# Second-layer weight preparation during the first MLP: later and spread slots, loads ahead of decoding, out weights decoded in place

## The chip, the cores and the metric

One core of a Trainium2 chip runs the whole program. The metric is the device time of one execution in microseconds; lower is better.

## What is computed

A linear attention with a normalised output, and behind it two MLPs on the same 2304 tokens:

```python
def _attn_ref(q, k, v, g_norm):            # q, k, v: (4, 8, 576, 64)
    kv = np.einsum('bhsd,bhse->bhde', k, v)
    out = np.einsum('bhsd,bhde->bhse', q, kv)
    rms = np.sqrt(np.mean(out * out, axis=-1, keepdims=True) + 1e-06)
    return (out / rms * g_norm).astype(np.float32)

def _moe_ref(x, w_in, w_out):              # x: (2304, 512), w_in: (512, 2048)
    h = x @ w_in
    sp = np.where(h > 20.0, h, np.log1p(np.exp(np.minimum(h, 20.0))))
    return ((h * np.tanh(sp)) @ w_out).astype(np.float32)

def _moe2_ref(x, w_in, w_out, alpha):      # the second MLP
    h = x @ w_in
    g = np.maximum(h, 0.0) + alpha * np.minimum(h, 0.0)
    return (g @ w_out).astype(np.float32)
```

The weights arrive as 64-bit floating-point numbers. q, k, v and the output are float32.

## The kernel before

Every product is made of three fp32r matmuls (`three`, L125): high part by high part, high by low, low by high. So each operand is needed as a high part (a cast on ACT) and a low part (a subtraction on DVE).

**Slots.** The first MLP runs over five blocks of tokens (`BLOCKS`, 512, 256, 512, 512, 512) and 16 tiles j of the inner dimension, in NS = 80 slots; slot s is block s // 16, tile s % 16. In a slot PE makes the first product of s (`mm1`, 12 matmuls, tile h), ACT the Mish of s - 1 (`mish`, L502), ACT and DVE the two parts of its result (`g_split`, L495 and L496, tiles gh and gl) for s - 2, and PE the second product of s - 4 (`mm2`, 12 matmuls, tile acc). The attention of block i + 1 is strewn between these on half slots (`WHEN`, the dictionary `hook`): k by v, q by kv, mean squares, the rsqrt chain (`rsqrt_ev`, L319 to L330, 12 operations on DVE and one cast on ACT, tiles qT and yr), and `b_pe` (L336), which spreads yr over the partitions. PE's `b_pe` of blocks 2, 3 and 4 stands in slots 28, 44 and 60, and the chain starts two and a half to three slots before.

**The second MLP** runs in 96 quarters after slot 79 (slot NS + n is quarter n), three passes over 768 tokens of eight units each. A unit is two tiles j of the inner dimension, whose first product is computed with seven instead of eight block products, from sums and differences of the weights. Those, and all second-layer weights, are prepared while the first MLP runs:

- `load_w` loads a tile of 64-bit words into a stage buffer (512 KB). `w_scale` (L387, ACT) and `w_bits` (L393, L394 and L397, DVE) decode it to float32 in a buffer `wf` of which there are two.
- `prep_unit(i, step)`, in slots from `UNITS[i]` on: two decodes, four operations on 256 columns (L597 to L602), and five splits (`whole`, `high_low`, L572 and L573); the store of each result to a DRAM tile `wd` (`put`, L581) follows right behind it.
- `prep_out(j)`, in slot `OUTS[j]`: one decode, one split, one store.
- `fetch` (L624) brings the stored tiles back into the places of the first layer's weights when these have been used for the last time, `load_s` (L628) the sums and differences, unit by unit.

There are three stage buffers (tag `ws`, `stage`). They serve second-layer loads, the results of a unit (`wx`, two of them), the first MLP's results on their way to DRAM (`evac`, `xs`, two at each block's end) and the second MLP's inputs on their way back (`first_raw`, `xr`). `first_x` (L669 and on) splits these for the first pass, into tiles that `rooms1` takes from the two buffers of the tag `x`, which until then hold the blocks' inputs.

**What sets the order.** `add` puts a call into a dictionary under a slot, and `slot` runs `early`, `mm1`, `hook`, `after`, `late`, the rest of the slot's products, `mid`, `fin`, and at its end `last`. Up to slot 19 this order is the order of every queue. From slot 20 on only PE's order is written out; for ACT, DVE and SP, which issues every DMA, it is a priority, and a scheduler that runs when the program is built sets the order of each queue. Each queue then runs in that fixed order.

Of the kernel before, what the change touches and what calls it, by code (L numbers as in the profile page):

```python
# [25 lines left out]
P = 128  # L26
# [7 lines left out]
EARLY = 4  # L34
WHEN = {1: (8, 3, 1, 2, 3, 6), 2: (4, 4, 1, 2, 3, 6), 3: (0, 5, 1, 2, 4, 5), 4: (0, 5, 1, 2, 4, 5)}
MANUAL = 20
UNITS = (28, 31, 36, 39, 42, 45, 52, 55)
OUTS = (24, 25, 26, 27, 34, 48, 49, 50, 58, 59, 60, 61, 62, 63, 64, 65)
BY32 = 2
FIRST = "p0 c0 p1 c1 p2 p3 c2 c3 w4 u0 w5 u1".split()  # L40
START = """
# [8 lines left out]
def attn_moe_moe2(  # L50
# [89 lines left out]
    def room(nm, dt, cols):  # L140
        w, j = rooms.pop(0)
        return wp.tile([P, 2 * DM], dt, tag=f"w{w}{j}", name=nm)[:, :cols]
# [219 lines left out]
    def stage(nm, dt, cols):  # L362
        return st.tile([P, 2 * DM], dt, tag="ws", name=nm, bufs=3)[:, :cols]
# [3 lines left out]
    wst, wraw = {}, {}  # L367
    home = {}

    def load_w(L, which, j, early=False):  # L370


        s = room("ws", I32, 2 * DM) if early else stage("ws", I32, 2 * DM)
        if which == 2:
            nc.sync.dma_start(out=s, in_=wo[L][j * P : (j + 1) * P, :])
        elif which == 1:
            src = wi[L][:, 2 * j * P : 2 * (j + 1) * P].rearrange("(c p) f -> p c f", p=P)
            nc.sync.dma_start(out=s.rearrange("p (c f) -> p c f", c=NP), in_=src)
        else:
            nc.sync.dma_start(out=s, in_=wi[L][j * P : (j + 1) * P, : 2 * EARLY * P])  # L380
        wraw[L, which, j] = s
        words = s.rearrange("p (f w) -> p f w", w=2)
        wst[L, which, j] = words[:, :, 0], words[:, :, 1]
# [2 lines left out]
        high = f32(wst[L, which, j][1])  # L386
        nc.scalar.mul(high, high, 2.0**-112)  # L387

    def w_bits(L, which, j):
        low, high = wst[L, which, j]  # L390
        s = st.tile([P, DM], F32, tag="wf", name="wf")
        si = s.bitcast(I32)
        nc.vector.tensor_single_scalar(out=si, in_=low, scalar=29, op=ALU.logical_shift_right)  # L393
        nc.vector.scalar_tensor_tensor(  # L394
            out=si, in0=high, scalar=-0x80000000, in1=si, op0=ALU.bitwise_and, op1=ALU.bitwise_or
        )
        nc.vector.scalar_tensor_tensor(  # L397
            out=si, in0=high, scalar=3, in1=si, op0=ALU.logical_shift_left, op1=ALU.bitwise_or
        )
        wst[L, which, j] = s  # L400
# [178 lines left out]
    def put(nm, t):  # L579
        d = wd[nm] = dp.tile([P, t.shape[1]], F32, name="wd")  # L580
        nc.sync.dma_start(out=d, in_=f32(t))  # L581

    def prep_unit(i, step):

        j0, j1 = 2 * i, 2 * i + 1
        tt = nc.vector.tensor_tensor
        if step < 2:
            j = j0 + step
            w_scale(1, 1, j)
            w_bits(1, 1, j)  # L590
            return
        sa, sb = wst[1, 1, j0], wst[1, 1, j1]
        r0, r1 = wraw[1, 1, j0], wraw[1, 1, j1]
        s1, s3 = (f32(r1)[:, n * QW : (n + 1) * QW] for n in range(2))
        a11, a12, a21, a22 = sa[:, :QW], sa[:, QW:], sb[:, :QW], sb[:, QW:]
        if step == 2:
            tt(out=s1, in0=a21, in1=a22, op=ALU.add)  # L597
            tt(out=s3, in0=a11, in1=a21, op=ALU.subtract)
            tt(out=a21, in0=s1, in1=a11, op=ALU.subtract)
            whole(r0, sa)  # L600
            put((1, j0), r0)
            tt(out=a12, in0=a12, in1=a21, op=ALU.subtract)  # L602
            high_low(*halves(r1, 1), s1)
            put(("s", i, 1), r1[:, 2 * QW :])
        else:
            x = stage("wx", I32, 2 * DM)
            high_low(*halves(x, 0), s3)
            put(("s", i, 0), x[:, : 2 * QW])
            high_low(*halves(x, 1), a12)
            put(("s", i, 2), x[:, 2 * QW :])  # L610
            x = stage("wx", I32, 2 * DM)
            whole(x, sb)
            put((1, j1), x)

    def prep_out(j):
        w_scale(1, 2, j)
        w_bits(1, 2, j)
        r = wraw[1, 2, j]
        whole(r, wst[1, 2, j])
        put((2, j), r)  # L620

    def fetch(which, j):
        h, l = w_home(1, which, j)
# [185 lines left out]
    def add(d, s, f, *a):  # L809
        d.setdefault(s, []).append((f, a))  # L810
# [35 lines left out]
    for j in range(NJ):  # L846
        if j >= EARLY and (1, j) not in early_w:
            add(late, max(j - 3, EARLY), load_w, 0, 1, j)
            add(mid, j - 2, w_begin, 0, 1, j)
        if (2, j) not in early_w:  # L850
            add(early, max(j + 1, EARLY), load_w, 0, 2, j)
            add(last, j + 2, w_begin, 0, 2, j)
            add(mid, j + 3, w_end)
        add(early, NS - NJ + max(j, EARLY) + 1, fetch, 1, j)
        add(early, NS + 2 * j - 3, fetch, 2, j)
    for i, s in enumerate(UNITS):
        for step in range(4):
            add(fin, s + step - step // 2, prep_unit, i, step)
        for n in range(2):
            add(last, s - 1, load_w, 1, 1, 2 * i + n)  # L860
    for j, s in enumerate(OUTS):
        add(fin, s, prep_out, j)
        add(last, s - 1, load_w, 1, 2, j)
    add(early, NS - NJ + 4, rooms1)
    for n in range(2):
        add(early, NS - 6 + 3 * n, first_raw, n)
        add(fin, NS - 5 + 3 * n, first_x, n)
    add(early, NS, rooms2)
    for n in range(3):
        add(early, NS, load_s, 0, n)  # L870
# [158 lines left out]
```

## Time and profile before

| | |
|---|---|
| median of three runs | 905.21 us (898.15 to 906.84) |
| the profiled execution | 907.59 us, of which span 905.8 us |
| PE busy | 849.1 us, 94% |
| DVE busy | 551.7 us, 61% |
| ACT busy | 318.0 us, 35% |
| mean granted TensorE clock | 0.976 |

The span runs from the first to the last instruction of one profiled execution; the rest of its time lies around it. Busy shares are means over stages that differ much. A wait is put down to the instruction that ended it. `ws<-in_moe_w_in_dram` reads: tile ws is written from the weights in DRAM; SPq is the queue that issues DMAs. The granted clock is a share of 2.4 GHz; TensorE runs either at that or at 1.2 GHz.

### The profile page before, as it was taken

What the parts mean: (1) busy time and instruction counts of PE and PEld (TensorE: products, weight loads), DVE (VectorE), ACT (ScalarE), POOL (GpSimd) and SP (SyncE); (2) the same over time, 40 slices, a digit from 0 to 9 for tenths busy, and PEclk for the clock granted to TensorE, in tenths of its full rate; (3) what the DMA queues carried; (4) which work ended last, traced back from release to release, by engine and by line L of the source; (5) the groups of instructions that cost most, each with busy time, mean ns of one, the idle gap of its engine ahead of it and who ended that gap; (6) DMA issues with size and microseconds to landing.
All of it is one profiled execution on the core that took longest, in us unless ns stands there. A gap on an engine that the chain in (4) does not pass through costs nothing.

```text
span 905.8 us, 11722 instructions
## 1 busy us (share of the span) xinstructions
PE 849.1 (94%) x4408; PEld 721.4 (80%) x4408; DVE 551.7 (61%) x1062; ACT 318.0 (35%) x619; POOL 1.3 (0%) x7
## 2 busy tenths in 40 slices
PE   7999889868996999959999999999999999999997
PEld 5677678757875788748888888888889888898886
DVE  6988864685548826682251355557855559655554
ACT  4766444544454435442242211112311114211111
POOL 0000000000000000000000000000000000000000
PEclk9999999969999999979999999999999999999999
DMA  9676446946574615650485641232412132211211
GB/s 263 182 201 178 134 117 172 258 159 147 165 237 151 184 61 198 243 187 24 160 284 195 209 151 48 57 91 62 128 47 59 47 117 59 104 59 48 59 47 70
DMA packets 89352, 121.37 MB, mean 134 GB/s; under 512 B 35280, under 2 KB 59344, under 8 KB 89296
## 3 DMA queue, kind: packets, MB, share of 16 engines
q1 hardware_dynamic: 89296, 120.62, 43.3%
q8 instruction: 35, 0.57, 0.3%
q14 instruction: 21, 0.17, 0.1%
HBM read 88.09 MB, written 32.51 MB: 133 GB/s over the span
## 4 chain that ended last, share of the span: by engine, by line
PE 65%; DMA 16%; DVE 12%; ACT 3%; SPq 2%; issue 2%; DVEq 0%; ACTq 0%
PE acc L129 11%; PE acc L127 11%; PE acc L128 11%; PE pp L127 6%; PE pp L129 6%; PE pp L128 6%; PE h L127 4%; PE h L128 4%; PE h L129 4%; DMA ws<-in_moe_w_in_dram 3%; DMA ws<-in_moe_w_out_dram 3%; DMA wd<-wx 3%; DMA wd<-ws 2%; DMA xr<-x2d 2%; DMA q<-in_q_dram 2%
## 5 line engine op out<-in xcount | busy, mean ns | idle before, releaser
L127 PE MATMUL acc<-gh,w 128*128 128x512 f32 (+1 forms) x320 | 122.5, 383 | 0.9 <-ACT n L502 0.4
L128 PE MATMUL acc<-gl,w 128*128 128x512 f32 (+1 forms) x320 | 120.5, 376 | 0.0
L129 PE MATMUL acc<-gh,w 128*128 128x512 f32 (+1 forms) x320 | 120.4, 376 | 0.0
L127 PE MATMUL h<-x,w 128*128 128x512 f32 (+1 forms) x240 | 93.7, 391 | 12.0 <-ACT n L502 12.0
L496 DVE TENSOR_TENSOR gl<-n,gh 128x512 fp32r<-128x512 f32 (+1 forms) x80 | 50.7, 633 | 82.4 <-ACT gh L495 82.3
L129 PE MATMUL h<-x,w 128*128 128x512 f32 (+1 forms) x240 | 90.9, 379 | 0.4 <-DVE w L436 0.3
L128 PE MATMUL h<-x,w 128*128 128x512 f32 (+1 forms) x240 | 90.7, 378 | 0.0
L129 PE MATMUL acc<-w,g 128*128 128x512 f32 x216 | 85.6, 396 | 0.2
L734 ACT CAST g<-ty 128x384 fp32r<-128x384 f32 x48 | 24.7, 514 | 150.0 <-DVE ty L732 140.9
L127 PEld LDWEIGHTS acc<-gh,w 128*128 128x128 f32 x320 | 62.6, 196 | 12.3 <-ACT n L502 0.9
L495 ACT CAST gh<-n 128x512 fp32r<-128x512 f32 (+1 forms) x80 | 46.1, 576 | 72.6 <-PE acc L129 72.1
L129 PEld LDWEIGHTS acc<-gh,w 128*128 128x128 f32 x320 | 62.3, 195 | 10.9 <-DVE w L436 0.4
L128 PEld LDWEIGHTS acc<-gl,w 128*128 128x128 f32 x320 | 62.6, 196 | 10.1
L127 PEld LDWEIGHTS h<-x,w 128*128 128x128 f32 x240 | 47.1, 196 | 25.7 <-ACT n L502 15.5
L387 ACT ACTIVATE ws<-ws 128x512 f32<-128x512 f32 x64 | 43.6, 683 | 54.7 <-DMA ws<-in_moe_w_in_dram 28.1
L128 PE MATMUL acc<-w,xb 128*128 128x512 f32 x144 | 56.8, 395 | 0.0
L128 PE MATMUL acc<-w,g 128*128 128x512 f32 x144 | 56.8, 395 | 0.0
L393 DVE TENSOR_SCALAR wf<-ws 128x512 int32<-128x512 int32 x64 | 27.1, 424 | 48.3 <-DMA ws<-in_moe_w_in_dram 24.9
L502 ACT ACTIVATE n<-h 128x512 f32<-128x512 f32 (+1 forms) x80 | 44.4, 555 | 33.2 <-DVE gl L496 32.4
L127 PE MATMUL acc<-w,g 128*128 128x512 f32 x144 | 56.0, 389 | 0.0
L127 PE MATMUL acc<-w,xb 128*128 128x512 f32 x144 | 56.0, 389 | 0.0
L129 PEld LDWEIGHTS h<-x,w 128*128 128x128 f32 x240 | 47.1, 196 | 9.4 <-DVE w L436 1.6
(183 smaller groups left out, 1702.4 us busy)
## 6 DMA issues: line engine op xcount, KB each, us to landing
xb<-wd SPq DMA_DIRECT2D x72, 256.0 KB, 2.7
ws<-in_moe_w_in_dram SPq DMA_DIRECT2D x32, 512.0 KB, 4.3
ws<-in_moe_w_out_dram SPq DMA_DIRECT2D x32, 512.0 KB, 4.1
w<-wd SPq DMA_DIRECT2D x28, 512.0 KB, 3.6
wd<-ws SPq DMA_DIRECT2D x24, 512.0 KB, 2.7
k<-in_k_dram SPq DMA_DIRECT2D x16, 288.0 KB, 4.6
v<-in_v_dram SPq DMA_DIRECT2D x16, 288.0 KB, 4.9
out_dram<-osb SPq DMA_DIRECT2D x18, 256.0 KB, 2.2
```

The lines of the kernel that those rows point to most:

```text
L127: nc.tensor.matmul(ps, lh, rh, start=start, stop=False, **kw)
L128: nc.tensor.matmul(ps, lh, rl, start=False, stop=False, **kw)
L129: nc.tensor.matmul(ps, ll, rh, start=False, stop=stop, **kw)
L387: nc.scalar.mul(high, high, 2.0**-112)
L393: nc.vector.tensor_single_scalar(out=si, in_=low, scalar=29, op=ALU.logical_shift_right)
L495: nc.scalar.copy(out=gh, in_=g)
L496: nc.vector.tensor_tensor(out=gl, in0=g, in1=f32(gh), op=ALU.subtract)
L502: nc.scalar.activation(out=g, in_=hps.pop(kk)[:, :T], func=AF.Mish)
L734: nc.scalar.copy(out=h, in_=out)
```

## The change

It moves the preparation of the second layer's weights and takes one part of it out of DRAM.

- Units are spread: `UNITS` starts at slots 36, 41, 46, 52, 57, 62, 65 and 70 instead of 28 to 55. The loads of a unit's two tiles stand in slots s and s + 1 (`late`, in the middle of the slot), their decodes in s + 1 and s + 2, the rest in s + 2 to s + 4, each store one slot after what it stores. Before, both loads stood at the end of slot s - 1 and the work in s to s + 2.
- A unit uses three stage buffers instead of four uses of them: the split of its second tile goes where that of its first was (`place`). Units 6 and 7 use neither stage buffers nor `wf`, but one of the two buffers of tag `x` (`late_places`); `rooms1` moves from slot 68 to 75, the first pass's input loads from 74 and 77 to 75 and 77, its splits from 75 and 78 to 76 and 78.
- Out tiles are loaded into the place where the second MLP reads them, once the first layer's tile there has been used (`load_out`, from slot 70 on), and decoded there two slots later (`prep_w`). There is no store and no fetch for them, and eight of the sixteen come after slot 80. `OUTS` and `prep_out` go.

```diff
@@ -34,8 +34,8 @@
 EARLY = 4
 WHEN = {1: (8, 3, 1, 2, 3, 6), 2: (4, 4, 1, 2, 3, 6), 3: (0, 5, 1, 2, 4, 5), 4: (0, 5, 1, 2, 4, 5)}
 MANUAL = 20
-UNITS = (28, 31, 36, 39, 42, 45, 52, 55)
-OUTS = (24, 25, 26, 27, 34, 48, 49, 50, 58, 59, 60, 61, 62, 63, 64, 65)
+SOON = 6
+UNITS = (36, 41, 46, 52, 57, 62, 65, 70)
 BY32 = 2
 FIRST = "p0 c0 p1 c1 p2 p3 c2 c3 w4 u0 w5 u1".split()
 START = """
@@ -367,10 +367,10 @@
     wst, wraw = {}, {}
     home = {}
 
-    def load_w(L, which, j, early=False):
-
-
-        s = room("ws", I32, 2 * DM) if early else stage("ws", I32, 2 * DM)
+    def load_w(L, which, j, early=False, s=None):
+
+
+        s = s if s is not None else room("ws", I32, 2 * DM) if early else stage("ws", I32, 2 * DM)
         if which == 2:
             nc.sync.dma_start(out=s, in_=wo[L][j * P : (j + 1) * P, :])
         elif which == 1:
@@ -386,9 +386,9 @@
         high = f32(wst[L, which, j][1])
         nc.scalar.mul(high, high, 2.0**-112)
 
-    def w_bits(L, which, j):
+    def w_bits(L, which, j, s=None):
         low, high = wst[L, which, j]
-        s = st.tile([P, DM], F32, tag="wf", name="wf")
+        s = s if s is not None else st.tile([P, DM], F32, tag="wf", name="wf")
         si = s.bitcast(I32)
         nc.vector.tensor_single_scalar(out=si, in_=low, scalar=29, op=ALU.logical_shift_right)
         nc.vector.scalar_tensor_tensor(
@@ -580,17 +580,36 @@
         d = wd[nm] = dp.tile([P, t.shape[1]], F32, name="wd")
         nc.sync.dma_start(out=d, in_=f32(t))
 
+    places, late_places = {}, {}
+
+    def place(i, nm):
+
+        if (i, nm) not in places:
+            if i < SOON:
+                t = stage(nm, I32, 2 * DM) if nm in ("r0", "r1", "x") else st.tile([P, DM], F32, tag="wf", name="wf")
+            else:
+                if not late_places:
+                    t = xp.tile([P, 8 * TM], I32, tag="x", name="xw")
+                    for n, to in enumerate(("r0", "r1", "x")):
+                        late_places[to] = t[:, 2 * n * DM : 2 * (n + 1) * DM]
+                    for n, to in enumerate("ab"):
+                        late_places[to] = f32(t[:, (6 + n) * DM : (7 + n) * DM])
+                t = late_places[nm]
+            places[i, nm] = t
+        return places[i, nm]
+
+    def load_unit(i, n):
+        load_w(1, 1, 2 * i + n, s=place(i, f"r{n}"))
+
     def prep_unit(i, step):
 
-        j0, j1 = 2 * i, 2 * i + 1
+        if step < 2:
+            j = 2 * i + step
+            w_scale(1, 1, j)
+            w_bits(1, 1, j, place(i, "ab"[step]))
+            return
         tt = nc.vector.tensor_tensor
-        if step < 2:
-            j = j0 + step
-            w_scale(1, 1, j)
-            w_bits(1, 1, j)
-            return
-        sa, sb = wst[1, 1, j0], wst[1, 1, j1]
-        r0, r1 = wraw[1, 1, j0], wraw[1, 1, j1]
+        sa, sb, r0, r1 = (place(i, nm) for nm in ("a", "b", "r0", "r1"))
         s1, s3 = (f32(r1)[:, n * QW : (n + 1) * QW] for n in range(2))
         a11, a12, a21, a22 = sa[:, :QW], sa[:, QW:], sb[:, :QW], sb[:, QW:]
         if step == 2:
@@ -598,26 +617,28 @@
             tt(out=s3, in0=a11, in1=a21, op=ALU.subtract)
             tt(out=a21, in0=s1, in1=a11, op=ALU.subtract)
             whole(r0, sa)
-            put((1, j0), r0)
+        elif step == 3:
+            x = place(i, "x")
             tt(out=a12, in0=a12, in1=a21, op=ALU.subtract)
             high_low(*halves(r1, 1), s1)
+            high_low(*halves(x, 0), s3)
+            high_low(*halves(x, 1), a12)
+        else:
+            whole(r0, sb)
+
+    def put_unit(i, step):
+        r0, r1, x = (places.get((i, nm)) for nm in ("r0", "r1", "x"))
+        if step == 0:
+            put((1, 2 * i), r0)
+        elif step == 1:
             put(("s", i, 1), r1[:, 2 * QW :])
+            put(("s", i, 0), x[:, : 2 * QW])
+            put(("s", i, 2), x[:, 2 * QW :])
         else:
-            x = stage("wx", I32, 2 * DM)
-            high_low(*halves(x, 0), s3)
-            put(("s", i, 0), x[:, : 2 * QW])
-            high_low(*halves(x, 1), a12)
-            put(("s", i, 2), x[:, 2 * QW :])
-            x = stage("wx", I32, 2 * DM)
-            whole(x, sb)
-            put((1, j1), x)
-
-    def prep_out(j):
-        w_scale(1, 2, j)
-        w_bits(1, 2, j)
-        r = wraw[1, 2, j]
-        whole(r, wst[1, 2, j])
-        put((2, j), r)
+            put((1, 2 * i + 1), r0)
+
+    def load_out(j):
+        load_w(1, 2, j, s=wp.tile([P, 2 * DM], I32, tag=f"w2{j}", name="ws"))
 
     def fetch(which, j):
         h, l = w_home(1, which, j)
@@ -852,19 +873,20 @@
             add(last, j + 2, w_begin, 0, 2, j)
             add(mid, j + 3, w_end)
         add(early, NS - NJ + max(j, EARLY) + 1, fetch, 1, j)
-        add(early, NS + 2 * j - 3, fetch, 2, j)
+        t0 = NS - 10 + 3 * j // 2 if j < 8 else NS + 2 * (j - 7)
+        add(early, t0, load_out, j)
+        add(fin, t0 + 2, prep_w, 1, 2, j)
     for i, s in enumerate(UNITS):
-        for step in range(4):
-            add(fin, s + step - step // 2, prep_unit, i, step)
-        for n in range(2):
-            add(last, s - 1, load_w, 1, 1, 2 * i + n)
-    for j, s in enumerate(OUTS):
-        add(fin, s, prep_out, j)
-        add(last, s - 1, load_w, 1, 2, j)
-    add(early, NS - NJ + 4, rooms1)
+        add(late, s, load_unit, i, 0)
+        add(late, s + 1, load_unit, i, 1)
+        for step in range(5):
+            add(fin, s + (1, 2, 2, 3, 4)[step], prep_unit, i, step)
+        for step in range(3):
+            add(late, s + 3 + step, put_unit, i, step)
+    add(early, NS - 5, rooms1)
     for n in range(2):
-        add(early, NS - 6 + 3 * n, first_raw, n)
-        add(fin, NS - 5 + 3 * n, first_x, n)
+        add(early, NS - 5 + 2 * n, first_raw, n)
+        add(fin, NS - 4 + 2 * n, first_x, n)
     add(early, NS, rooms2)
     for n in range(3):
         add(early, NS, load_s, 0, n)
```

## Rows read from the trace of the kernel before

**Rows 1.** The page's first line.

```profile
span 905.8 us, 11722 instructions
```

**Rows 2.** Busy by stretch: us; PE, weights, DVE, ACT, POOL busy (x); clock; DMA share, GB/s.

```profile
124.74:156.75 32.01, 31.00 (x252) 27.12 (x250) 17.13 (x31) 15.65 (x36) 0.00 (x0) 1.00 0.49 119
156.75:233.51 76.76, 59.70 (x419) 53.49 (x417) 48.32 (x95) 34.81 (x79) 0.00 (x0) 0.87 0.66 186
233.51:316.94 83.43, 75.04 (x362) 59.35 (x361) 59.94 (x114) 40.06 (x79) 0.00 (x0) 0.96 0.60 190
316.94:422.04 105.10, 94.59 (x409) 76.50 (x408) 59.68 (x106) 46.19 (x83) 0.00 (x0) 0.95 0.44 154
422.04:509.28 87.24, 87.24 (x385) 71.99 (x384) 23.23 (x40) 27.23 (x48) 0.00 (x0) 1.00 0.57 192
509.28:590.00 80.72, 80.72 (x401) 72.43 (x400) 44.05 (x83) 15.09 (x29) 0.00 (x0) 1.00 0.33 102
620.00:660.00 40.00, 39.61 (x195) 34.97 (x194) 33.39 (x68) 15.67 (x31) 0.00 (x0) 1.00 0.29 92
```

**Rows 3.** PE's waits, 156.75 to 233.51: total us, times, longest.

```profile
PE bps L336 <- DVE yr L330: 7.8, 1, 7.8
PE h L127 <- ACT n L502: 6.1, 4, 2.4
```

**Rows 4.** The same, 233.51 to 316.94.

```profile
PE bps L336 <- DVE yr L330: 5.1, 1, 5.1
```

**Rows 5.** The same, 316.94 to 422.04.

```profile
PE bps L336 <- DVE yr L330: 9.3, 1, 9.3
```

**Rows 6.** DVE's busy time in the windows of two rsqrt chains.

```profile
276.00:294.00 18.00, 15.77 (x31) 0.94 0.52 179
...
379.50:400.00 20.50, 17.54 (x32) 0.86 0.62 218
```

**Rows 7.** The same for tile qT alone, the chain's operations.

```profile
276.00:294.00 18.00, 8.02 (x12) 0.94 0.52 179
...
379.50:400.00 20.50, 8.02 (x12) 0.86 0.62 218
```

**Rows 8.** Groups by line in these windows: xcount | busy, mean ns | idle before.

```profile
L393 DVE TENSOR_SCALAR wf<-ws 128x512 int32<-128x512 int32 x2 | 0.9, 428 | 2.1 <-DMA ws<-in_moe_w_in_dram 2.1
...
L393 DVE TENSOR_SCALAR wf<-ws 128x512 int32<-128x512 int32 x4 | 1.7, 426 | 3.0 <-DMA ws<-in_moe_w_out_dram 3.0
```

**Rows 9.** DVE's timeline: start, us, instruction, idle before it.

```profile
284.00 0.43 DVE L393 TENSOR_SCALAR wf<-ws 128x512 int32<-128x512 int32 x1 [1.09 <-DMA ws<-in_moe_w_in_dram]
284.35 0.68 DVE L325 SCALAR_TENSOR_TENSOR qT<-qT 128x512 f32<-128x512 f32 x1
```

**Rows 10.** Groups by line, whole run.

```profile
L394 DVE SCALAR_TENSOR_TENSOR wf<-ws,wf 128x512 int32<-128x512 int32 x64 | 44.2, 690 | 6.7 <-ACT ws L387 3.7
...
L393 DVE TENSOR_SCALAR wf<-ws 128x512 int32<-128x512 int32 x64 | 27.1, 424 | 48.3 <-DMA ws<-in_moe_w_in_dram 24.9 <-DMA ws<-in_moe_w_out_dram 23.3
...
L573 DVE TENSOR_TENSOR ws<-wf,ws 128x512 fp32r<-128x512 f32 x24 | 16.5, 688 | 3.2 <-ACT ws L572 3.0
...
L597 DVE TENSOR_TENSOR ws<-wf 128x256 f32<-128x256 f32 x8 | 3.4, 421 | 0.1
```

**Rows 11.** DMA issues of the page: count, KB each, median us to landing.

```profile
ws<-in_moe_w_in_dram SPq DMA_DIRECT2D x32, 512.0 KB, 4.3
ws<-in_moe_w_out_dram SPq DMA_DIRECT2D x32, 512.0 KB, 4.1
```

**Rows 12.** Waits of the whole run, DVE's decode for its loads.

```profile
DVE wf L393 <- DMA ws<-in_moe_w_in_dram: 24.9, 14, 4.9
...
DVE wf L393 <- DMA ws<-in_moe_w_out_dram: 23.3, 11, 7.4
```

**Rows 13.** SP's timeline: start, us, issues.

```profile
319.66 0.38 SPq L378 DMA_DIRECT2D ws<-in_moe_w_in_dram  x1
...
443.12 0.68 SPq L665 DMA_DIRECT2D xr<-x2d  x1
```

## The prediction

> **What bounds the kernel now.** I read the span first, and then a table of PE by stretches that I cut at the starts of slots, found in the timeline as the first product of a slot: 124.74 is slot 16, 156.75 slot 23, 233.51 slot 36, 316.94 slot 48, 422.04 slot 64, 509.28 the first product of the second MLP. I call the stretches A to F [rows 2]. The reader is to see three columns there: PE's busy time against the length, DVE's, and the granted clock.
>
> E is what an undisturbed stretch looks like: 16 slots in 87.24 us with PE busy for all of it and the clock at 1.00, so a slot of 512 tokens takes 5.45 us. A is nearly as clean, 1.0 us idle in 32.0. B, C and D are not. I count as lost there the idle time and the share of the stretch that the clock did not grant (a mean of 0.87 says that 13% of the cycles of the upper level, 2.4 GHz, were missing; the two overlap a little, so this is a slight overestimate). B: 76.76 - 59.70 = 17.1 idle and 0.13 x 76.76 = 10.0 of clock, 27 us. C: 8.4 and 3.3, 11.7 us. D: 10.5 and 5.3, 15.8 us. Together 54.5 of the 905.8 us span [rows 1]. The change can only work on these 54.5 us: it removes no work from PE.
>
> Next I asked who ended PE's waits. One wait of 7.8 us in B, one of 5.1 us in C and one of 9.3 us in D are the same place, b_pe (L336), waiting for yr (L330), the end of the rsqrt chain of blocks 2, 3 and 4 [rows 3 to 5]. In B another 6.1 us are the first layer's product waiting for Mish, the longest 2.4 us [rows 3]. So DVE and ACT are late, not PE, and the clock that B, C and D lose follows those idle stretches.
>
> Why is yr late? Between 276 and 294 us DVE spent 8.02 us on the 12 operations of the chain, but 15.77 us on everything; between 379.5 and 400 us 8.02 of 17.54 us [rows 6, 7]. The rest is almost all decoding of second-layer weights, placed between the chain's operations: L393 at 284.00, then L325 of the chain right behind it [rows 9]. And L393 stood in line for its load: 2.1 us in the first of these windows, 3.0 us in the second [rows 8]. DVE works in its order, so the chain waits as well. Over the whole run L393 waited 48.2 us in 25 waits for loads, 1.9 us each [rows 12].
>
> **What the change does, part by part.**
>
> *Work.* Nothing leaves DVE or ACT. A weight tile's decode stays L393, L394, L397 (the last is of the same kind and size as L394) and a split: 0.42 + 2 x 0.69 + 0.69 = 2.5 us of DVE for an out tile. A unit is two decodes (3.6 us), two splits at full width (1.4) and seven operations on 256 columns (7 x 0.42 = 2.9): 7.9 us of DVE [rows 10]. What goes away is DMA: 16 stores of decoded out tiles and their 16 fetches, with 16 uses of the three shared stage buffers. PE waits for none of these fetches where it waits long [rows 3 to 5], so their price on the path is zero; what they occupied is the buffers, SP's queue and bandwidth.
>
> *Where the work goes.* Units leave slots 28 to 57 for 36 to 74, outs leave 24 to 65 for 72 to 98. B (slots 23 to 35) held four outs, units 0 and 1 and a fifth out, and is left with at most the first load and decode of unit 0. So in B the chain stands alone. It needs 8 us, and the three slots of 256 tokens between its first operation and b_pe give about that (3 x 5.45 / 2 = 8.2); the 7.8 us wait falls away, and with it the 2.4 us wait for Mish and the clock lost after them. I keep A's idle rate (1.0 / 32.0 of 76.76 us, 2.4 us) and the other 3.7 us of waits for Mish, which stand around the loads of q and not only around the decodes. 27.1 - 6.1 = 21 us gained in B. Ends: 27 if those waits go too, 15 if the clock's share comes back only by half and 1 us of the chain's wait stays.
>
> *C and D.* Here I don't take the new slot numbers at their word. They order the work, but only PE's order is written out; on the other queues a step starts when its buffer is free. first_raw is listed for slot 74 and its first load issued at 443.12, in slot 67 (438.4 to 443.8 by 5.45 us a slot); a unit's load listed for slot 51 issued at 319.66, in slot 48 [rows 13]. So I expect units 0 to 2 to follow each other from slot 36 as fast as three buffers allow, and units 3 to 5 from slot 52, and both later chains (slots 41 to 44 and 57 to 60) to meet a unit again. What gets better: loads stand further ahead of decodes, so I take off L393's waits in those windows, 2.1 of the 5.1 us in C and 3.0 of the 9.3 us in D. In D a unit also replaces outs running back to back, and DVE's other work shrinks towards that of C: (17.54 - 8.02) - (15.77 - 8.02) = 1.8 us. With the clock in proportion to the idle time that makes 2.1 x (1 + 3.3 / 8.4) = 2.9 us in C and 4.8 x (1 + 5.3 / 10.5) = 7.2 us in D. Ends: nothing in either, and all but 1 us of each, 10.7 and 14.8.
>
> A load takes 4.3 and 4.1 us in the median to land [rows 11], within a slot of 5.45, but the waits [rows 8, 12] show that the issue came too late for that. The Trainium skill's page "DMA: Bandwidth & Descriptors", section "Anatomy of one DMA", gives 2.0 us and the bytes over 436 GB/s for another queue than SP's; an estimate by it is 3.2 us for 512 KB. By that rule half a slot of lead is enough, a longer one buys nothing, and the sum would lose the DMA part of C and D, 2.9 and 4.5 us, for a time near 885. The loads here are slower than the rule and the waits are there, so I go by the trace.
>
> *Puts and order on SP.* The puts come a slot after what they store. SP then waits less for DVE, and the loads behind a put issue sooner; this is in the 2.1 and 3.0 us above. A unit now uses three stage buffers and writes its last split over the first, so that split waits for a store to land, on DVE; nothing but the unit needs it, and its slot (s + 4) is two behind the store's work.
>
> *E and F pay.* Three units less what runs ahead, some eight outs and first_x come into E, where DVE is busy 23.23 of 87.24 us: 3 x 7.9 + 8 x 2.5 = 44 us more, 77%. E has no rsqrt chain. Units 6 and 7 hold an x buffer, so the split of the second MLP's inputs cannot run as early as it did; it must now fit between the last store of unit 7 and slot 80, and what is late next would be the second MLP's first products. The other eight outs, 20 us of DVE, come into the second MLP, which is busy 44.05 of 80.72 us there: 64 of 81, 79%. The nearest row is 620 to 660, DVE 33.39 of 40.00 us, PE idle 0.4 us in 40 [rows 2]. By that F loses 0.8 us. If the cover of E and F were gone, each of 22 loads would cost PE its 1.9 us, 42 us and more with the clock. I take 3 us, near the row: 1 in F, 2 for the transition.
>
> **Sum.** 21 + 2.9 + 7.2 - 3 = 28 us. The profiled execution took 907.59 us, 905.8 of span and 1.8 around it; the median of the runs is 2.4 us lower, 905.2. So 879.6 for an execution like the profiled one, and 877 on the median.
>
> **Rivals.**
>
> 1. *All comes back* (0.20). The units do spread as listed, a chain meets one decode at most, and the two and a half slots from its first operation to b_pe (13.6 us) are enough. B + C + D: 21 + 10.7 + 14.8 - 3 = 43 us, 862. For it: the chain alone needs 8 of these 13.6 us. Against it: issues that run ahead of their slots [rows 13].
> 2. *The later chains are as late as before* (0.14). Units from slots 36 and 52 crowd DVE as they did, loads are late again, and only B gains: 21 - 3 = 18, 887. For it: DVE in C, where only units ran and it was busy for 15.77 us of 18 [rows 6].
> 3. *The other side: E and F become what B was* (0.07). Decodes wait for their loads in front of operations that PE needs soon. One such wait costs 1.9 us and, with B's clock over idle time, 1.9 x (1 + 10.0 / 17.1) = 3.0 us. From ten of them on (31 us of gain over 3.0) the change is slower; 16, one for each out, give 905 - 31 + 48 = 922. Against it: E without idle time, and two slots of lead.
> 4. *It doesn't do what it says* (0.09). The scheduler puts each decode right behind its load again, B fills with work pulled forward (attention's loads, unit 0), and what is gained in one chain is lost at the transition: 905.
>
> **How the numbers follow.** The forecast has 0.50, with a range of its own from 868 to 886. Left out may be 0.2: I leave out most of 3 and 4 and the far end of 1, and get 856 to 896. This kernel's three runs reach from 898 to 907, so about 1% (9 us) is what can be told from no change. Faster by over 1% (below 896): forecast, 1 and 2, 0.84 less a little for their upper ends, 0.83. Within 1%: 4 and the mild end of 3, 0.10. Slower: 0.07.
>
> **What would show it.** Right, if PE's wait at L336 in slot 28 is under 1 us and the clock there stays near 1.00; if slots 23 to 35 take about 56 us instead of 76.76; if the waits at L336 in slots 44 and 60 are there but under 3 and 5 us; if L393's waits for loads fall well below 48 us; if there is no store or fetch of out tiles, and PE is idle less than 4 us more in slots 64 to 98. Wrong, if the waits in slots 44 and 60 are as long as before (rival 2) or gone (rival 1), or if PE waits in the first quarters of the second MLP for operations that stand behind a decode (rival 3).

## The result, and the profile after

The median falls from 904.33 us (898.15 to 906.84, four runs) to 870.04 us (869.05 to 872.79, four runs): a ratio of 0.964, 95% interval 0.961 to 0.968, 34.3 us less. The profiled execution took 872.79 us. The page's first line and its row of the granted clock:

```profile
span 870.8 us, 11649 instructions
...
PEclk9999899999999999999999999999999999999999
```

The same row of the kernel before:

```profile
PEclk9999999969999999979999999999999999999999
```

The span is 35.0 us shorter than in [rows 1], and the two slices in which the clock had been low, around 190 and 396 us, are full; the 8 that stands now belongs to 87 to 109 us, in the first block's slots, which the change doesn't touch. Busy time by stretch, cut at the same slots as [rows 2] (slots 16, 23, 36, 48, 64, the second MLP's first product): us; PE, weights, DVE, ACT, POOL busy (x); clock; DMA share, GB/s. The stretches are A, B, C, D, E, and the last is the second MLP's first 80.72 us:

```profile
126.73:160.38 33.65, 31.10 (x251) 27.12 (x249) 18.25 (x33) 16.04 (x37) 0.00 (x0) 1.00 0.53 116
160.38:214.63 54.25, 51.70 (x419) 47.22 (x417) 24.83 (x44) 21.69 (x54) 0.00 (x0) 1.00 0.29 63
214.63:293.11 78.48, 74.26 (x362) 58.83 (x360) 47.72 (x87) 32.90 (x66) 0.00 (x0) 0.98 0.45 143
293.11:387.02 93.91, 92.54 (x410) 75.04 (x409) 49.50 (x89) 39.91 (x74) 0.00 (x0) 1.00 0.30 101
387.02:474.68 87.66, 87.66 (x385) 71.85 (x384) 60.46 (x113) 45.50 (x83) 0.00 (x0) 1.00 0.72 254
474.68:555.40 80.72, 79.81 (x394) 71.11 (x393) 53.94 (x103) 21.47 (x40) 0.00 (x0) 1.00 0.31 102
```

B is 22.5 us shorter, C 5.0, D 11.2; E is as long as it was, with DVE busy for 60.46 us of it instead of 23.23; and the second MLP from its first product to the end took 396.2 us, before 396.5. Against that stand 2.0 us more up to slot 16 and 1.6 us more in A, where nothing was changed. 22.5 + 5.0 + 11.2 - 3.6 = 35.1, the span's difference but for rounding.

PE's waits of the whole run (total us, times, longest):

```profile
PE h L127 <- ACT n L502: 7.5, 8, 1.9
PE bps L336 <- DVE yr L330: 5.3, 3, 2.1
```

The three waits at b_pe were 7.8, 5.1 and 9.3 us [rows 3 to 5]; now they are 1.9 in slot 28, 2.1 in slot 44 and 1.3 in slot 60. The chains of blocks 3, 4 and 2, in this order, from their first operation to the end of yr, before and then after (columns as above; a chain is 12 operations of DVE):

```profile
276.48:293.30 16.82, 9.64 (x42) 7.30 (x40) 14.61 (x29) 6.41 (x13) 0.00 (x0) 0.95 0.53 180
379.68:399.80 20.12, 9.66 (x42) 7.34 (x40) 17.16 (x32) 7.96 (x14) 0.00 (x0) 0.86 0.62 218
175.66:194.30 18.64, 8.74 (x59) 8.33 (x57) 16.35 (x33) 7.33 (x16) 0.00 (x0) 0.77 0.53 167
```

```profile
259.77:271.30 11.53, 9.34 (x40) 7.07 (x39) 11.22 (x21) 4.52 (x10) 0.00 (x0) 1.00 0.33 126
355.66:366.85 11.19, 9.85 (x43) 7.50 (x41) 10.87 (x20) 4.23 (x8) 0.00 (x0) 1.00 0.32 119
172.88:183.40 10.52, 8.73 (x72) 8.53 (x72) 9.20 (x15) 3.10 (x8) 0.00 (x0) 1.00 0.01 2
```

The two later chains took 16.8 and 20.1 us with 15 and 18 foreign operations between their own, and now take 11.5 and 11.2 with 8 and 7 (the counts of these windows hold one or two more, at the edges). That of block 2 took 18.6 us and takes 10.5, with three operations of `g_split` left in it and no unit. DVE's timeline shows where the foreign operations stand in block 3's chain (start, us, instruction):

```profile
259.77 0.69 DVE L319 TENSOR_SCALAR qT<-msps 128x512 f32<-128x512 f32 x1
260.38 0.42 DVE L618 TENSOR_TENSOR wf<-r,wf 128x256 f32<-128x256 f32 x1
260.71 0.42 DVE L573 TENSOR_TENSOR r<-r 128x256 fp32r<-128x256 f32 x1
...
263.25 0.42 DVE L573 TENSOR_TENSOR x<-wf,x 128x256 fp32r<-128x256 f32 x1
263.59 0.69 DVE L325 SCALAR_TENSOR_TENSOR qT<-qT 128x512 f32<-128x512 f32 x1
...
270.52 0.75 DVE L330 SCALAR_TENSOR_TENSOR yr<-yr,neglo,qT 128x512 fp32r<-128x512 f32 x1
```

Up to 263.6 the end of unit 2 alternates with the chain as a unit did before; from there on the chain meets only two of `g_split`'s operations (L496). SP's timeline says why (start, us, issues):

```profile
248.12 1.83 SPq L378 DMA_DIRECT2D r<-in_moe_w_in_dram  x2
...
274.84 6.45 SPq L180 DMA_DIRECT2D q<-in_q_dram  x8
281.33 0.49 SPq L378 DMA_DIRECT2D r<-in_moe_w_in_dram  x1
...
317.97 0.37 SPq L378 DMA_DIRECT2D r<-in_moe_w_in_dram  x1
```

Unit 2's loads, listed for slots 46 and 47, issued in slot 41, so its decode fell on the chain. Unit 3's first load came only in slot 45, behind the chain. Unit 2's stores had all landed by 267.0 us, but in SP's queue eight loads of q stood in front of it, which had waited for DVE (L243). Nothing else was there to decode: the outs that once filled this room now issue from slot 69 on.

### The profile page after: what moved, and what is told of

Same layout as the page of the kernel before. It is cut to its first block, busy times and chain, and to the rows that moved or that the text cites. A ratio compares the mean times of both kernels' runs of the same rounds, so it can differ in the third digit from the quotient of the medians.

```text
span 870.8 us, 11649 instructions
## 1 busy us (share of the span) xinstructions
PE 840.4 (97%) x4408; PEld 714.1 (82%) x4408; DVE 554.5 (64%) x1062; ACT 316.3 (36%) x619; POOL 1.3 (0%) x7
## 4 chain that ended last, share of the span: by engine, by line
PE 70%; DVE 14%; DMA 9%; ACT 3%; issue 2%; SPq 1%; DVEq 0%; ACTq 0%
PE acc L128 11%; PE acc L127 11%; PE acc L129 11%; PE pp L127 6%; PE pp L129 6%; PE pp L128 6%; PE h L127 5%; PE h L128 5%; PE h L129 5%; DMA r<-in_moe_w_in_dram 3%; DMA v<-in_v_dram 2%; DVE wf L394 2%; DVE wf L397 2%; PE kvps L211 1%; DMA wd<-x 1%
## 5 line engine op out<-in xcount | busy, mean ns | idle before, releaser
L127 PE MATMUL acc<-gh,w 128*128 128x512 f32 (+1 forms) x320 | 120.8, 377 | 0.6 <-ACT n L502 0.4
L129 PE MATMUL acc<-gh,w 128*128 128x512 f32 (+1 forms) x320 | 118.8, 371 | 0.0
L127 PE MATMUL h<-x,w 128*128 128x512 f32 (+1 forms) x240 | 91.7, 382 | 5.8 <-ACT n L502 5.7
L129 PE MATMUL h<-x,w 128*128 128x512 f32 (+1 forms) x240 | 89.8, 374 | 0.7 <-DVE w L436 0.7
L128 PE MATMUL h<-x,w 128*128 128x512 f32 (+1 forms) x240 | 89.3, 372 | 0.0
L496 DVE TENSOR_TENSOR gl<-n,gh 128x512 fp32r<-128x512 f32 (+1 forms) x80 | 50.7, 634 | 44.4 <-ACT gh L495 44.0
L127 PEld LDWEIGHTS acc<-gh,w 128*128 128x128 f32 x320 | 61.0, 190 | 11.9 <-ACT n L502 0.9
L129 PEld LDWEIGHTS acc<-gh,w 128*128 128x128 f32 x320 | 60.9, 190 | 10.8 <-DVE w L436 0.4
L495 ACT CAST gh<-n 128x512 fp32r<-128x512 f32 (+1 forms) x80 | 46.1, 576 | 52.9 <-PE acc L129 52.3
L127 PEld LDWEIGHTS h<-x,w 128*128 128x128 f32 x240 | 45.6, 190 | 18.9 <-ACT n L502 8.7
L129 PEld LDWEIGHTS h<-x,w 128*128 128x128 f32 x240 | 45.7, 191 | 9.4 <-DVE w L436 1.6
L128 PEld LDWEIGHTS h<-x,w 128*128 128x128 f32 x240 | 45.7, 190 | 7.2
L129 PEld LDWEIGHTS acc<-w,g 128*128 128x128 f32 x216 | 40.5, 188 | 9.6 <-DVE g L756 1.1
```

The source lines that it names most:

```text
L127: nc.tensor.matmul(ps, lh, rh, start=start, stop=False, **kw)
L128: nc.tensor.matmul(ps, lh, rl, start=False, stop=False, **kw)
L129: nc.tensor.matmul(ps, ll, rh, start=False, stop=stop, **kw)
L495: nc.scalar.copy(out=gh, in_=g)
L496: nc.vector.tensor_tensor(out=gl, in0=g, in1=f32(gh), op=ALU.subtract)
```

## Experiments

Three theories stood. *The lead*: loads stand ahead of decodes, so DVE waits less in front of the chain. *The chains' company*: what counts is which foreign operations stand between a chain's operations, whoever put them there. *The amount*: slots 23 to 63 simply held too much preparation of all kinds, and any thinning helps. (What an expectation calls its theory and its rival, it says itself.) The lengths below are differences between the starts of first products in the profiled executions; the medians are of all runs, and before is taken anew beside each group (904.8, 903.7 and 902.9 us). A profiled execution can lie off its median: that of 5 is the slowest of six (894.6 us), those of 6 (863.1) and of the kernel after (872.8) the slowest of four. Where the intervals of two kernels overlap, the medians alone don't tell them apart.

| kernel | median us | ratio, 95% | B | C | D | E | F |
|---|---|---|---|---|---|---|---|
| before | 904.3 | | 76.8 | 83.4 | 105.1 | 87.2 | 396.5 |
| after | 870.0 | 0.961 to 0.968 | 54.3 | 78.5 | 93.9 | 87.7 | 396.2 |
| 1 outs at home, old units | 887.6 | 0.978 to 0.984 | 67.1 | 81.5 | 92.1 | 87.6 | 397.2 |
| 2 the same, new unit slots | 869.7 | 0.959 to 0.968 | 55.4 | 74.6 | 94.1 | 87.1 | 400.6 |
| 3 after, no lead | 867.9 | 0.956 to 0.962 | 54.3 | 74.9 | 94.1 | 88.1 | 398.2 |
| 4 after, units behind chains | 862.6 | 0.951 to 0.957 | 54.4 | 73.1 | 92.0 | 87.8 | 396.6 |
| 5 before, all behind chains | 887.6 | 0.978 to 0.984 | 64.1 | 84.2 | 99.2 | 92.2 | 394.9 |
| 6 as 4, b_pe of block 2 later | 860.1 | 0.950 to 0.955 | 51.7 | 72.2 | 92.0 | 88.1 | 397.2 |
| 7 after, 8 outs decoded twice | 873.4 | 0.964 to 0.969 | 55.8 | 77.4 | 94.3 | 88.0 | 401.3 |
| 8 after, two units decoded twice | 876.4 | 0.968 to 0.973 | 54.7 | 80.2 | 96.4 | 88.3 | 396.6 |
| 9 before, L387 on GpSimd | 904.3 | 1.000 to 1.004 | 73.5 | 85.3 | 105.2 | 87.0 | 395.3 |
| 10 as 5, L387 on GpSimd | 887.9 | 0.981 to 0.986 | 63.8 | 84.8 | 98.2 | 87.2 | 395.4 |
| 11 as 6, L387 on GpSimd | 867.7 | 0.958 to 0.963 | 51.7 | 74.5 | 92.0 | 89.9 | 400.8 |

**1. Only the outs.** The kernel before, with second-product weights loaded to their place and decoded there late; units as they were.

```diff
...
+    def load_out(j):
+        load_w(1, 2, j, s=wp.tile([P, 2 * DM], I32, tag=f"w2{j}", name="ws"))
...
-        add(early, NS + 2 * j - 3, fetch, 2, j)
+        t0 = NS - 10 + 3 * j // 2 if j < 8 else NS + 2 * (j - 7)
+        add(early, t0, load_out, j)
+        add(fin, t0 + 2, prep_w, 1, 2, j)
...
-    for j, s in enumerate(OUTS):
-        add(fin, s, prep_out, j)
-        add(last, s - 1, load_w, 1, 2, j)
```

> The kernel before with one part of the change: out tiles are loaded and decoded in place, late; units keep their old slots, loads and four stage uses. Theory (work in front of the rsqrt chains): the outs leave stretches B and D, units 0 and 1 stay in B. PE's wait at L336 in slot 60 goes (9.3 us before) with its clock, some 13 us; B gains some 5 us from the outs that stood before slot 28; the waits in slots 28 and 44 stay at 3 to 8 us. About 886 us (880 to 893). Rival (DMA traffic and stage buffers are what costs, and this part takes away all the traffic that the change takes away): as the whole change, 870 to 874. Rival (the lead of the loads): nothing of it is in this kernel, over 898.

PE's waits at b_pe, whole run:

```profile
PE bps L336 <- DVE yr L330: 11.7, 2, 6.6
```

6.6 us in slot 28, 5.1 in slot 44, none in slot 60. Half of the gain, 17 of 34 us, is the outs', 13 us of the profiled execution's in D, where outs had stood in the chain of block 4, and 10 in B. The rival, by which the traffic that is gone brings the whole gain, is refuted; but decodes, traffic and buffers of the outs go together here, and this run does not part them. C keeps its wait, as it should: units 2 to 5 still fill it.

**2. New unit slots besides.** One line more; a unit's loads, its four buffers and its steps as before.

```diff
-UNITS = (28, 31, 36, 39, 42, 45, 52, 55)
+UNITS = (36, 41, 46, 52, 57, 62, 68, 71)
```

> Outs in place as in the first run, and units in the new slots (36, 41, 46, 52, 57, 62, then 68 and 71), but with the old unit: both loads in the slot before the first decode, stores right behind the work, four uses of the three stage buffers. Theory (where the work stands is what counts): B is clear, 868 to 876, at most 5 us over the changed kernel since a unit with four buffer uses takes longer and meets the chain of slot 44 for longer. Rival (lead, stores a slot later and three buffers carry the gain of the later stretches): 880 to 888.

```profile
PE bps L336 <- DVE yr L330: 5.0, 3, 1.9
```

The other half: 869.7, B and C 12 and 7 us shorter than in experiment 1. This kernel has the old lead, one slot, and the old units, and is as fast as the change. Its second MLP took 400.6 us, some 4 us more than in the kernel after; that was not followed up.

**3. No lead.** The kernel after, with loads listed in the slot of their decode.

```diff
-        add(early, t0, load_out, j)
+        add(early, t0 + 2, load_out, j)
...
-        add(late, s, load_unit, i, 0)
-        add(late, s + 1, load_unit, i, 1)
+        add(late, s + 1, load_unit, i, 0)
+        add(late, s + 2, load_unit, i, 1)
```

> The changed kernel with every load of a unit and of an out tile listed in the slot of its own decode instead of one or two slots before. Theory (slots only order the work, a load issues when its buffer is free, so the listed lead hardly moves the issues): as the changed kernel, 868 to 873, decodes wait for loads as long as there. Rival (the lead is what keeps decodes from standing in front of the chains): L393's waits for loads go up by 1 to 2 us each and the time to 876 to 885.

SP's timeline, the loads of units 2 (both) and 3:

```profile
241.42 1.82 SPq L378 DMA_DIRECT2D r<-in_moe_w_in_dram  x2
...
273.07 0.49 SPq L378 DMA_DIRECT2D r<-in_moe_w_in_dram  x1
...
309.71 0.37 SPq L378 DMA_DIRECT2D r<-in_moe_w_in_dram  x1
```

Counted in slots that is 41, 45.9 and 52.3, the very places of the kernel after. Here the listed slot doesn't set the issue. Unit 2's two loads issue when stores of unit 1 have landed, unit 3's first behind loads of q in SP's queue, its second when a store of `evac` has landed. With the same queue the time is no longer than the change's. So the lead in the list is not a cause. What a longer lead in fact would bring is not tried by this.

**4 and 6. The chains alone.** In 4, the DVE operations of units 2 and 5, which fall on the chains of blocks 3 and 4, are put behind yr; in 6, b_pe of block 2, with no unit in its chain, also comes half a slot later.

```diff
+HOLD = {2: 3, 5: 4}
...
-            nc.vector.scalar_tensor_tensor(
+            at["end", i] = nc.vector.scalar_tensor_tensor(
...
+        if i in HOLD:
+            with tc.issue_after(at["end", HOLD[i]].ins):
+                unit_step(i, step)
```

```diff
-WHEN = {1: (8, 3, 1, 2, 3, 6), 2: (4, 4, 1, 2, 3, 6), 3: (0, 5, 1, 2, 4, 5), 4: (0, 5, 1, 2, 4, 5)}
+WHEN = {1: (8, 3, 1, 2, 3, 6), 2: (4, 4, 1, 2, 3, 7), 3: (0, 5, 1, 2, 4, 5), 4: (0, 5, 1, 2, 4, 5)}
```

> The changed kernel, with the DVE operations of unit 2 put behind the last operation of block 3's rsqrt chain (L330) and those of unit 5 behind that of block 4. Theory (what is left of the waits in slots 44 and 60 is a unit's operations between the chain's): the waits of about 2 us and 1 to 2 us there and the half-speed stretch behind the first go, 864 to 867. Rival (the chain is too long for its slots by itself, or its input is late): the waits stay, 869 to 872.

> The kernel of e4_hold with block 2's four b_pe half a slot later (58 to 61 half slots instead of 57 to 60). Theory (the 1.9 us of wait left in slot 28 are the chain's own length against three slots of 256 tokens): the wait goes to under 1 us, 1 to 2 us faster than e4_hold, 861. Rival (what makes it late is ahead of the chain): as e4_hold, 862 to 863.

PE's wait at b_pe in 4 (lines are one further down), and the two later chains in 6:

```profile
PE bps L337 <- DVE yr L331: 1.9, 1, 1.9
```

```profile
252.46:262.10 9.64, 9.64 (x44) 8.00 (x43) 8.64 (x15) 3.07 (x5) 0.00 (x0) 1.00 0.00 0
344.68:354.30 9.62, 9.62 (x44) 7.98 (x43) 8.62 (x15) 3.00 (x5) 0.00 (x0) 1.00 0.01 2
```

With no unit in it, a later chain takes 9.6 us and PE does not stop for it; for block 2's, half a slot later, PE still stops 0.5 us in 6. The waits of slots 44 and 60 were worth 7 us to the change, somewhat more than expected. That of slot 28 brought another 2.5 by the medians; the intervals of 4 and 6 overlap, but B is 2.7 us shorter. Kernel 6, at 860.1 us, is the fastest here, 10 us or 1.1% below the change.

**5. The chains alone, in the kernel before.** All of `prep_unit` and `prep_out` on DVE behind the end of the last chain that stands earlier in the list; amount and slots as before.

```diff
...
+    def behind(f, *args):
+        with tc.issue_after(ends[-1].ins):
+            f(*args)
...
-            add(fin, s + step - step // 2, prep_unit, i, step)
+            add(fin, s + step - step // 2, behind, prep_unit, i, step)
...
-        add(fin, s, prep_out, j)
+        add(fin, s, behind, prep_out, j)
```

> The kernel before, nothing moved and nothing decoded in place: only an order is added, by which the DVE operations of every unit step and out tile that is listed behind a block's rsqrt chain also stand behind the chain's last operation (L330) in DVE's queue. Theory (the gain of the change is that less preparation stands between the chain's operations): the waits at L336 in slots 28, 44 and 60, 22.2 us, fall to some 2, 2 and 3 us, the clock stays up behind them, and the time comes most of the way to the changed kernel, 872 to 882 us. Rival (the amount of second-layer work, its transfers and its stage buffers in the first MLP are what costs): no more than half of that, over 888, since the held work piles up behind the chains and Mish waits for it.

PE's waits, whole run (lines are two further down):

```profile
PE h L127 <- ACT n L504: 17.5, 14, 3.6
PE acc L127 <- ACT xs L516: 7.7, 1, 7.7
...
PE bps L338 <- DVE yr L332: 1.9, 1, 1.9
```

The 22.2 us of waits at b_pe become 1.9 us, and yet the time falls by 16 us only, to just short of the rival's 888. What was held back is late elsewhere: in the profiled execution C doesn't gain and E loses 5 us. The 7.7 us stand in slot 36, where block 2's results go into stage buffers. ACT's timeline (idle time and what ended it in brackets):

```profile
232.00 0.67 ACT L389 ACTIVATE ws<-ws 128x512 f32<-128x512 f32 x1 [4.46 <-DMA ws<-in_moe_w_out_dram]
232.60 0.37 ACT L516 COPY xs<-acc 128x256 f32<-128x256 f32 x1
233.77 0.37 ACT L516 COPY xs<-acc 128x256 f32<-128x256 f32 x1 [0.81 <-DMA wd<-wx]
```

The copy that frees PE's accumulators stood behind a scaling that waited for its load. So freeing the chains alone, with all work and all transfers still in these slots, brings about half of the gain. The other half came only with less work there; what of that work costs it (DVE's time, ACT's, the transfers or the stage buffers) is not shown.

**7 and 8. The amount, by doubling.** In 7 the decode of the eight outs behind slot 80 is done twice on DVE (14.4 us more, from slot 77 on, most of it in the second MLP); in 8 that of units 2 and 5 (3.6 us more beside each of the later chains).

```diff
...
-        add(fin, t0 + 2, prep_w, 1, 2, j)
+        add(fin, t0 + 2, prep_w if j < 8 else prep_twice, 1, 2, j)
```

```diff
+            raw = wst[1, 1, j]
             w_bits(1, 1, j, place(i, "ab"[step]))
+            if i in (2, 5):
+                wst[1, 1, j] = raw
+                w_bits(1, 1, j, place(i, "ab"[step]))
```

> The changed kernel, where the eight out tiles that are listed behind slot 80 are decoded twice: 8 x 1.8 = 14.4 us more on DVE, in slots 76 to 84. It prices the cover of the work that the change moved there. Theory (DVE has room there, and PE needs nothing soon of what stands behind the decodes): at most 2 us slower than the changed kernel, 869 to 872. Rival (the moved work is at the edge of what the transition and the second MLP can hide): 875 to 885.

> The changed kernel, where the four weight tiles of units 2 and 5 are decoded twice: 4 x 1.8 = 7.2 us more on DVE, half of what e7_outs_twice adds, but in the units that run into the chains of slots 44 and 60. Theory (what stands between the chain's operations delays it by its own length): the waits there go from 2.1 and 1.3 us to some 5 each and the clock falls behind them, 877 to 883. Rival (DVE is busy for 60% and takes it in its idle time): under 873.

PE's waits: 7, from the end of slot 79 on; then 8, whole run:

```profile
PE pp L127 <- ACT tx L809: 3.0, 1, 3.0
PE pp L127 <- DVE ty L763: 1.6, 2, 1.2
```

```profile
PE bps L336 <- DVE yr L330: 9.2, 3, 4.6
```

8 came close to its theory: 4.6 and 2.7 us in slots 44 and 60 instead of 2.1 and 1.3, where some 5 each were expected, and 876.4 us in all where 877 to 883 were. It is 6.4 us more than the change, 3.2 for each 3.6 us of DVE beside a chain. The clock fell behind the wait in slot 44 alone (0.50 there, 1.00 behind slot 60). 7 lies between its two expectations: 3.4 us more by the medians where 2 at most were expected. The intervals of 7 and the change overlap, but PE waits 4.6 us in the second MLP instead of 1.4. So the second MLP covers most of a doubled decode of the outs, not all.

**9 to 11. The ACT part elsewhere.** The scaling of second-layer words (L387) on GpSimd, in the kernel before, in 5 and in 6.

```diff
-        nc.scalar.mul(high, high, 2.0**-112)
+        if L:
+            nc.gpsimd.tensor_scalar(out=high, in0=high, scalar1=2.0**-112, scalar2=None, op0=ALU.mult)
+        else:
+            nc.scalar.mul(high, high, 2.0**-112)
```

> The kernel before, with one operation moved to another engine: the scaling of second-layer weights (L387, the first to wait for a load) runs on GpSimd, which does nothing else, instead of ACT. Theory A (part of the loss in the first MLP is ACT standing in front of a load with Mish, the results' copies and yr's cast behind it): PE's 16 us of waits for Mish fall by half or more, 885 to 897 us. Theory B (DVE alone is what is late; L393 waits for the same loads there): no change, 900 to 908, or slower, if GpSimd's operation is slow and DVE's L394 waits for it instead.

> The kernel of e5_before_hold with the same move to GpSimd. In e5_before_hold the chains were free and 15.0, 14.3 and 7.9 us were still lost in slots 23 to 35, 36 to 47 and 48 to 63, among it 7.7 us in slot 36, where a scaling on ACT waited 4.5 us for a load in front of the block's copies. Theory A: with ACT free of loads most of this goes, 868 to 880. Theory B (the amount of work held back behind the chains is too much for the slots that are left): as e5_before_hold, 884 to 892.

> The kernel of e6_hold_later_b with the same move to GpSimd. Little is left there in the first MLP behind slot 22 (6 us) and 4 us of it are waits for Mish: theory A expects 856 to 859, theory B 860 or slower.

9 is as fast as before, as theory B had it: the waits for Mish fall from 16.0 to 12.0 us, those at b_pe rise from 22.2 to 23.8. In 10, PE's waits and, around slot 36, ACT's:

```profile
PE h L127 <- ACT n L507: 11.8, 9, 2.7
PE acc L127 <- ACT xs L519: 7.3, 1, 7.3
```

```profile
232.31 0.37 ACT L519 COPY xs<-acc 128x256 f32<-128x256 f32 x1 [2.98 <-DMA wd<-wx]
```

The time is that of 5. The waits for Mish are 6 us shorter, but the wait of slot 36 is nearly as long: without the scaling in front, the copy waits for the store of a unit's result to leave the stage buffer it needs. So ACT's place in line was not the cause in 5, or not the only one: the shared stage buffers are enough. 11 is 7.6 us slower than 6: C 2.3, E 1.8 and F 3.6 us in the profiled execution. GpSimd's groups by line there (xcount | busy, mean ns | idle before), and a row of its timeline:

```profile
L389 POOL TENSOR_SCALAR ws<-ws 128x512 f32<-128x512 f32 x16 | 36.6, 2292 | 56.5 <-DMA ws<-in_moe_w_out_dram 56.5
L389 POOL TENSOR_SCALAR r<-r 128x512 f32<-128x512 f32 x12 | 20.2, 1693 | 323.0 <-DMA x2d<-xs 211.7 <-DMA r<-in_moe_w_in_dram 101.7 <-DVE qs L247 9.6
```

```profile
487.67 3.68 POOL L389 TENSOR_SCALAR ws<-ws 128x512 f32<-128x512 f32 x1 [3.37 <-DMA ws<-in_moe_w_out_dram]
```

The operation that ACT does in 0.68 us takes 1.5 to 2.1 here, and for three of the out tiles 3.7 to 6.5. DVE's decode waits for the one of 3.68 us with the second MLP's operations in line behind, and PE stands for 4.1 us, from 490.3 to 494.4.

## Why the prediction was right, and where it was not

The forecast was 877, the time is 870, inside the likeliest case's own range (868 to 886). The mechanism given for B held. For C and D the sum was 6 us too low and the reason given fell in part. That the total still lies in the range is in part luck: the range was wide enough for the miss. Step by step, by what the profiled executions show:

- **B, 21 us forecast, 22.5 measured.** The mechanism is the one given: units and outs gone, the chain of block 2 runs alone, the clock stays at 1.00. Two signs were a little off: slots 23 to 35 took 54.25 us where about 56 was named, and the wait in slot 28 is 1.9 us, not under 1. The step that failed there is "it needs 8 us, and the three slots of 256 tokens give about that": 8.0 us is what DVE is busy with the chain, but from its first operation to the end of yr it took 10.5 us with no unit in it. So it is 1.9 us too late for b_pe, and in experiment 6 half a slot takes all but 0.5 of that away.
- **C and D, 2.9 and 7.2 forecast, 5.0 and 11.2 measured.** The picture was right: the loads run ahead of their slots and both chains meet a unit. The 2.1 and 3.0 us of waits for loads are gone from both chains, as reckoned. What was mis-sized is the rest, DVE's foreign work: I gave it nothing in C and 1.8 us in D. By the windows above DVE was busy 14.61 and 17.16 us in the chains and is now 11.22 and 10.87, 3.4 and 6.3 us less. In the old D those were outs back to back (experiment 1 alone takes 13 us there). In the new chains the second half is free, because the next unit is not there yet: unit 3's first load stands in SP's queue behind the loads of q, and those of unit 6 wait for an x buffer, which block 3's last product frees in slot 63 (384.5 us).
- **The reason given for it, that loads stand further ahead, fell.** L393's waits for loads were to fall well below 48 us [rows 12]. By tile they now are:

```profile
DVE wf L393 <- DMA r<-in_moe_w_in_dram: 23.4, 8, 5.2
DVE wf L393 <- DMA ws<-in_moe_w_out_dram: 13.0, 7, 4.2
DVE xw L393 <- DMA xw<-in_moe_w_in_dram: 9.6, 3, 5.5
DVE wf L393 <- DMA ws<-in_moe_w_in_dram: 3.1, 1, 3.1
```

  49.1 us, as much as before, and none of it in a chain. The waits moved to places where PE, as its waits show, loses little by them. The total of a wait said nothing; its place did. Experiment 3 then shows that the listed lead hardly reaches the queue. The Trainium skill's page "DMA: Bandwidth & Descriptors", section "Anatomy of one DMA", by which an estimated 3.2 of the 5.45 us of a slot are lead enough (a little over the half slot that I named), agrees with that in its consequence. No run here shows it as the reason: the loads issued in the same slots either way, and landed in 4.4 us in the median.
- **E and F, a cost of 3 us forecast, none measured.** PE has no idle time in E with DVE busy 69% (60.46 of 87.66 us). In the second MLP it waits 1.4 us where it waited 2.0. DVE's 53.94 us of the first 80.72 are fewer than the 64 that I had added up: the loads of the outs run ahead of their slots too, and eleven of the sixteen issue before the second MLP starts. The doubt was the right one all the same: experiment 7, with 14.4 us more, took 3.4 more by the medians.
- **Rivals.** That all comes back (862) is not what happened, but experiments 4 and 6 reach it (862.6, 860.1) by its own condition, chains that meet nothing. That the later chains stay as late (887) is refuted by 2.1 and 1.3 us; that E and F become what B was, by E; that the scheduler fills B again, by B.

What stays open: how much of experiment 5's shortfall is DVE's backlog, how much ACT's and how much the stage buffers. C took 78.5 us in the kernel after and 74.9 in experiment 3, whose loads issue in the same slots: 1.6 of these 3.6 us are the clock in slot 44 (below), and some 2 us lie in slots 37 and 38, after unit 0's first load, which landed after 8.1 us in the one execution and 5.2 in the other; that this is the cause is not shown. So the 5.0 us of C are probably the low end of what the change brings there.

## What to carry to other kernels

Look for the one dependent chain that the bounding engine waits for, and count what stands between its operations on its own queue. The units' work cost the more the more of it stood between these operations (waits of 0, 2.1 and 4.6 us in slot 44 with unit 2 held back, as it was, and decoded twice), and nothing measurable in the 16 slots behind the last chain, with that engine busy 69%. A slot in a list is no time of issue where a buffer, the queue in front or a scheduler decides; read the issues from the trace of before, and if an order matters, write it down as a dependence: for two units that was worth 7 us, and the lead that the lists asked for nothing.

## What the runs showed of the hardware

- The same short wait may or may not cost the clock. In the kernel after, PE's wait in slot 44 (2.12 us) was followed by a stretch at the lower of its two levels (1.2 GHz); in experiment 3 the same wait in the same slot (2.07 us) was not. Windows around it, in the kernel after and then in experiment 3 (the first window of each holds the wait, the second follows it):

```profile
268.00:271.70 3.70, 1.58 (x7) 1.05 (x6) 3.12 (x5) 1.20 (x2) 0.00 (x0) 1.00 0.00 0
271.70:275.20 3.50, 3.50 (x10) 2.69 (x9) 2.15 (x3) 0.62 (x1) 0.00 (x0) 0.51 0.02 5
```

```profile
261.30:265.00 3.70, 1.63 (x7) 1.05 (x6) 3.12 (x5) 1.20 (x2) 0.00 (x0) 1.00 0.00 0
265.00:268.50 3.50, 3.50 (x17) 2.83 (x16) 2.43 (x4) 1.13 (x2) 0.00 (x0) 1.00 0.02 5
```

  In the window of the wait the work of DVE and ACT is the same to the hundredth. At a clock of 0.51, 3.50 us of PE hold 10 products instead of 17, and slot 44 takes 9.99 us instead of 8.43. So the same wait cost about 2 us in one execution and about 3.6 in the other, and executions of one kernel may differ by as much. The wait of 1.89 us in slot 28 shows both as well: the 3.5 us behind it ran at a clock of 1.00 in the kernel after and at 0.52 in experiment 7.
- GpSimd took 1.69 us for a multiplication by a constant over 128x512 words in place (stride of two words) that takes ACT 0.68 (experiment 11, the units' loads). For the 16 out tiles the mean was 2.29: three took 3.68, 4.46 and 6.47.
